# Moving phi's q + 1 to POOL, q's PSUM copy to ACT and low parts to DVE in an attention-and-MLP kernel

## The chip, the cores and the metric

The kernel runs on one core of a Trainium2 chip. The metric is the device time of one execution in microseconds (us). The engines of the core work at the same time and take their own queues in order: PE (TensorE, matmuls and transposes), DVE (VectorE), ACT (ScalarE), POOL (GpSimd) and SP, which issues the loads and stores. An instruction that waits holds up everything behind it in its engine's queue.

## The reference

Inputs are float32; B, H, S, D = 4, 8, 576, 64. First comes causal attention mixed with a linear memory, then two MLPs with 512 x 2048 and 2048 x 512 weights over the 2304 tokens:

```python
scores = np.where(causal, -1e9, q @ k.T / sqrt(D))      # per batch and head
local = softmax(scores) @ v
q_p = phi(q)                                  # phi(x) = (x if x > 0 else exp(x) - 1) + 1
mem_out = (q_p @ M_prev) / (q_p @ z_prev + 1e-6)
x = g * mem_out + (1 - g) * local             # g = sigmoid(beta), one value per head
x = x.transpose(0, 2, 1, 3).reshape(B * S, H * D)
h = x @ w_in;  x = (h * tanh(softplus(h))) @ w_out         # first MLP
h = x @ w_in2; out = (h * sigmoid(h)) @ w_out2             # second MLP
```

## The kernel before

Attention goes by 16 pairs of heads. A pair loads q, k and v (two buffers each); PE transposes q and k through PSUM, and the copies out of PSUM make `kT` (ACT, `Tkh`) and `qT` (DVE, `Tqh`). Scores are made in four bands of rows (`s4` to `s1`, and `s0` for the first 64 rows). DVE adds the mask and finds the extremum (`r`, line 562), ACT takes the exponential with the sum as its accumulator (`e`, line 586), DVE takes two small steps on the sum (`a` at line 616, `d` at 618), POOL scales the probabilities (`n`, line 601). PE transposes them (`X`), ACT and DVE copy them out, and PE multiplies by v (`V`, line 674).

Beside this, the memory part makes phi(q) as min(exp(q), 1) against q + 1: `phe` (ACT, exp), `phu` (ACT, q + 1, line 512), `phf` (DVE, line 513), then `phz` (POOL, product with z, line 515), `phr` (DVE, its sum, line 517), three small DVE steps and `phm` (POOL, line 522).

Both MLPs work in split precision: an operand is held as a high part, which is a cast to fp32r on ACT, and a low part, which is the operand less the high part. A product is three matmuls (lines 843 to 845 and 880). The tokens are cut into 6 blocks of 384 and the inner width of 2048 into 16 slices, in 4 quarters of 4 slices. A unit is one slice of one block: `in` (12 matmuls), `si` (ACT, the activation, line 858), `gh` (ACT, its high part, line 859), `gl` (DVE, its low part, line 860), `out` (12 matmuls in the first MLP, 9 in the second, line 880). Between `in` and `out` of one unit PE does other units' matmuls; there are three PSUM banks for `in` and five for `out`. The sums of a quarter are drained to `xT` (ACT for the first quarter, DVE after that, line 897).

There are 64 weight pieces (two MLPs x 16 slices x in and out). The loaded weights are put through bit steps on DVE (`abs` and `b0` to `b3`, lines 761 to 776, 128 x 512), then `hi` on ACT (line 784) and `lo` on POOL (line 788). The first quarter of the first MLP has 8 pieces, and their buffers exist from the start; the buffers for the next pieces and for the blocks of x open when attention's buffers close. Low parts of x (`xl`, line 829) are on POOL, but for two on DVE; there are 24 for each MLP.

The order on every engine comes from a planner (`Steps.plan`), which goes through all steps with a duration and an engine for each, and takes the ready step with the earliest latest-start time. `PERIOD` sets the due times of the pairs, and `SHIFT` adds a fixed time to the latest start of whole groups of steps. The planned order is then written out; the chip keeps it on each engine.

Of the kernel before, what the change touches and what calls it, by code (L numbers as in the profile page):

```python
# [21 lines left out]
AF = mybir.ActivationFunctionType  # L22
# [229 lines left out]
def pair_steps():  # L252
# [2 lines left out]
    for nm, d in (("nk", 1.6), ("nq", 1.7), ("nv", 3.1)):  # L255
        E("ld" + nm, "S", d, [], 2.7)
    E("phe", "A", act(640, False), ["ldnq"])
    E("phu", "A", act(640, False), ["ldnq"])
    m.group("t", ("Tk", "P", 0.44, ["ldnk"]), [("Tkh", "A", act(512), ["Tk"])])
    E("phf", "D", dve(640), ["phe", "phu"])  # L260
    m.group("t", ("Tq", "P", 0.44, ["ldnq"]), [("Tqh", "D", dve(512), ["Tq"])])
    E("phz", "G", 1.57, ["phf"])
    E("phr", "D", dve(640), ["phz"])
    E("pha", "D", 0.08, ["phr"])
# [71 lines left out]
class Attn:  # L336
# [162 lines left out]
    def steps(self, p):  # L499
# [9 lines left out]
        mid = slice(ST, S)  # L509

        f["phe"] = lambda: nc.scalar.activation(self.get(p, "e"), s["nq"], AF.Exp)
        f["phu"] = lambda: nc.scalar.activation(self.get(p, "u"), s["nq"], AF.Identity, bias=1.0)
        f["phf"] = lambda: nc.vector.scalar_tensor_tensor(  # L513
            out=s["e"], in0=s["e"], scalar=1.0, in1=s["u"], op0=ALU.min, op1=ALU.max)
        f["phz"] = lambda: nc.gpsimd.tensor_tensor(
# [13 lines left out]
        f["Tp"] = lambda: T("e")  # L529

        f["Tkh"] = lambda: self.hi(G("kT")[:, mid], s["Tnk"])
        f["Tqh"] = lambda: self.vec(G("qT"), s["Tnq"])
        f["Tph"] = lambda: [self.hi(G("W0")[R[j], j, mid], s["Te"][R[j], :]) for j in range(2)]

        def Ts():
# [192 lines left out]
class Weights:  # L728
# [13 lines left out]
    def steps(self, n):  # L742
        job = self.jobs[n]
        ph, i, part = job
        nc = self.nc

        def s_load():
            t = self.stg.tile([P, DM, 2], I32, tag="stg", name="stg")
            src = self.pairs[ph][part].bitcast(I32)
            if part == 0:  # L750
                nc.sync.dma_start(
                    t.rearrange("p (c f) x -> p c (f x)", c=KC),
                    src[:, 2 * i * P:2 * (i + 1) * P].rearrange("(c p) f -> p c f", p=P))
            else:
                nc.sync.dma_start(t.rearrange("p f x -> p (f x)"), src[i * P:(i + 1) * P, :])
            self.raw[job] = t

        def s_abs():
            c = self.stg.tile([P, DM], F32, tag="val", name="val", bufs=self.VALS)
            self.val[job] = c  # L760
            nc.vector.tensor_scalar(
                c.bitcast(U32), self.raw[job][:, :, 1].bitcast(U32), 0x7FFFFFFF, None, op0=ALU.bitwise_and)

        def s_bits(n):
            t, c = self.raw[job], self.val[job]
            cu = c.bitcast(U32)
            lo, hi = t[:, :, 0].bitcast(U32), t[:, :, 1].bitcast(U32)
            if n == 0:
                nc.vector.tensor_scalar(c, c, LEAST, MOST, op0=ALU.max, op1=ALU.min)
            elif n == 1:  # L770
                nc.vector.tensor_scalar(cu, cu, 3, 0x3FFFFFFF, op0=ALU.logical_shift_left, op1=ALU.bitwise_and)
            elif n == 2:
                nc.vector.scalar_tensor_tensor(
                    out=cu, in0=lo, scalar=29, in1=cu, op0=ALU.logical_shift_right, op1=ALU.bitwise_or)
            else:
                nc.vector.scalar_tensor_tensor(  # L776
                    out=lo, in0=hi, scalar=0xC0000000, in1=cu, op0=ALU.bitwise_and, op1=ALU.bitwise_or)

        def s_hi():
            k = i % SLOTS  # L780
            pool = self.fix if k < GC else self.late
            w = pool.tile([P, 2, DM], F32R, tag=f"w{k}{part}", name=f"w{k}{part}")
            self.W[job] = w
            nc.scalar.copy(w[:, 0, :], self.raw[job][:, :, 0].bitcast(F32))  # L784

        def s_lo():
            w = self.W[job]
            nc.gpsimd.tensor_tensor(  # L788
                w[:, 1, :], self.raw[job][:, :, 0].bitcast(F32), w[:, 0, :].bitcast(F32), op=ALU.subtract)
        bits = {f"b{n}": lambda n=n: s_bits(n) for n in range(4)}  # L790
        return dict(ld=s_load, abs=s_abs, hi=s_hi, lo=s_lo, **bits)

    def register(self, m, due, last):

        m.cap.update({"W.raw": 2, "W.val": self.VALS})
        for n, job in enumerate(self.jobs):
            ph, i, part = job
            f = self.steps(n)
            k = i % SLOTS
            ring = f"W.{k}{part}"  # L800
            m.cap[ring] = 1
            J = lambda x: ("W", job, x)
            t = due(job)
            slow = 0.2 if ph == 0 and i < GC else 0.0
            for x, e, d, deps in (("ld", "S", 3.8, []), ("abs", "D", 0.465, ["ld"]), ("b0", "D", 0.465, ["abs"]),
                                  ("b1", "D", 0.465, ["b0"]), ("b2", "D", 0.735, ["b1"]), ("b3", "D", 0.78, ["b2"]),
                                  ("hi", "A", 0.57, ["b3"] + (["open1"] if k >= GC else [])),
                                  ("lo", "G", 1.38, ["hi"])):
                m.add(J(x), e, d + (slow if e == "D" else 0.0), [y if y == "open1" else J(y) for y in deps], f[x], t)
            m.hold("W.raw", job, [J("ld")], [J("lo")], order=n)  # L810
            m.hold("W.val", job, [J("abs")], [J("b3")], order=n)
            m.hold(ring, job, [J("hi")], last(job), order=n)


class Moe:
# [5 lines left out]
    def split_x(self, ph, t, kc):  # L821
# [4 lines left out]
            nc.scalar.copy(self.xh[t][:, kc], self.xT[:, kc, ts])  # L826

        def lo():
            self.lo_engine(ph, t, kc).tensor_tensor(  # L829
                self.xl[t][:, kc], self.xT[:, kc, ts], self.xh[t][:, kc].bitcast(F32), op=ALU.subtract)  # L830
        return hi, lo

# [67 lines left out]
        r = t * TB + d * P  # L900
        self.nc.sync.dma_start(self.out[r:r + P, :], self.part(1, t, d))

    def lo_engine(self, ph, t, kc):
        return self.nc.vector if ph == 0 and t == 0 and kc % 2 else self.nc.gpsimd

    def open(self, n):

        tc, ctx = self.tc, self.ctx
# [17 lines left out]
    def register(self, m, base, ends, step=4.17):  # L926
# [6 lines left out]
        for t in range(NB):  # L933
            for kc in range(KC):
# [1 line left out]
                f = self.split_x(0, t, kc)  # L936
                heads = [(b * KC + kc, v) for b in range(t * TB // SEQ, ((t + 1) * TB - 1) // SEQ + 1) for v in ends]
                m.add((k, "h"), "A", 0.413, ["open%d" % (t // 3)] + heads, f[0], due[0, t, 0])
                e = self.lo_engine(0, t, kc) is self.nc.gpsimd
                m.add((k, "l"), "G" if e else "D", 0.955 if e else 0.466, [(k, "h")], f[1], due[0, t, 0])  # L940
        for n, u in enumerate(U):
            ph, t, i = u
            g = i // GC
# [26 lines left out]
            if i % GC == GC - 1:  # L970
                for d in range(nd):
# [11 lines left out]
                    if g == NG - 1 and ph == 0:  # L983
                        f = self.split_x(1, t, d)
                        z = ("z", t, d)
                        m.add((z, "h"), "A", 0.413, [k], f[0], due[1, t, 0])
                        m.add((z, "l"), "G", 0.955, [(z, "h")], f[1], due[1, t, 0])
                    elif g == NG - 1:
                        m.add((k, "st"), "S", 0.5, [k], lambda t=t, d=d: self.store(t, d), due[u] + 4)

# [10 lines left out]
        self.w.register(m, wdue, wlast)  # L1001


PERIOD = 9.921
SHIFT = {
# [19 lines left out]
}  # L1025


# [75 lines left out]
```

## Time and profile before

| what | us |
|---|---|
| median of 3 executions | 1046.67 (1046.45 to 1046.94) |
| the profiled execution, its own time | 1046.64 |
| its span in the trace | 1044.8 |
| PE busy | 1015.3 |
| DVE busy | 584.3 |
| ACT busy | 461.5 |
| POOL busy | 291.6 |

The span runs from the first to the last instruction in the trace, and 1.84 us of the execution lie around it. Busy times of several engines overlap. Matmuls are pipelined, so that a busy PE is not always PE at its peak rate. In an instruction's row `out<-in` gives the tiles by their names, and the brackets at its end hold the engine's idle time just before it and what ended that.

### The profile page before, as it was taken

The page shows a single profiled execution, that of the slowest core. Times are in us where ns is not written, and L with a number is a line of the kernel's source. Part 1 is how long each engine was busy: PE and PEld are TensorE (multiplying, and loading weights), DVE is VectorE, ACT ScalarE, POOL GpSimd, SP SyncE. Part 2 cuts the span into 40 slices and gives each one's busy share as a digit, 9 for nine tenths or more (in the row PEclk, how much of TensorE's full clock was granted, in tenths as well). Part 3 has the DMA queues.
Part 4 walks back from the last instruction along what each step waited for, and adds up shares of the span by engine and source line. Part 5 has one row for each costly group of instructions (what it writes and reads, how often), then busy time and mean ns, then how long its engine had stood idle before and what let it go on. Part 6 is the DMA issues. An engine that isn't in the chain of part 4 may idle for free.

```text
span 1044.8 us, 15751 instructions
## 1 busy us (share of the span) xinstructions
PE 1015.3 (97%) x5824; PEld 902.3 (86%) x5824; DVE 584.3 (56%) x1398; ACT 461.5 (44%) x1071; POOL 291.6 (28%) x303
## 2 busy tenths in 40 slices
PE   6999999988999999999999999999999999999998
PEld 4666666677999999999999999899999999998897
DVE  6999999999724732672278238512752372212222
ACT  6899898983424322332234334324422332222221
POOL 4887778787201200210024234101200120000000
PEclk9999999999999999999999999999999999999999
DMA  6433343122302300220031002100300120000011
GB/s 135 101 92 82 92 102 93 46 67 68 102 1 61 101 1 1 82 81 1 1 101 61 1 21 81 61 1 21 118 24 1 41 81 1 1 1 31 31 61 61
DMA packets 85309, 55.03 MB, mean 53 GB/s; under 512 B 61936, under 2 KB 78320, under 8 KB 85232
## 3 DMA queue, kind: packets, MB, share of 16 engines
q1 hardware_dynamic: 84032, 53.73, 18.2%
q8 instruction: 46, 0.75, 0.3%
q10 hardware_dynamic: 1200, 0.30, 0.1%
q14 instruction: 31, 0.25, 0.1%
HBM read 49.29 MB, written 4.72 MB: 52 GB/s over the span
## 4 chain that ended last, share of the span: by engine, by line
PE 80%; DVE 10%; POOL 4%; ACT 3%; issue 2%; DMA 1%; SPq 0%; POOLq 0%; ACTq 0%; DVEq 0%
PE acc L880 37%; PE hp L843 12%; PE hp L844 12%; PE hp L845 12%; DVE sm L562 3%; POOL xl L829 2%; PE ps_x L674 2%; PE ps_s L569 2%; DVE h L484 2%; ACT P L586 2%; PE ps_t L638 1%; DVE z L616 1%; DVE e L513 1%; PE ps_t L489 1%; DMA nq<-in_q_dram 1%
## 5 line engine op out<-in xcount | busy, mean ns | idle before, releaser
L858 ACT ACTIVATE a<-hp 128x384 f32<-128x384 f32 x192 | 94.5, 492 | 469.5 <-PE hp L845 469.4
L860 DVE TENSOR_TENSOR gl<-a,gh 128x384 fp32r<-128x384 f32 x192 | 116.4, 606 | 320.6 <-ACT gh L859 320.1
L843 PE MATMUL hp<-xh,w 128*128 128x384 f32 x768 | 258.9, 337 | 0.0
L844 PE MATMUL hp<-xl,w 128*128 128x384 f32 x768 | 258.5, 337 | 0.0
L845 PE MATMUL hp<-xh,w 128*128 128x384 f32 x768 | 258.5, 337 | 0.0
L788 POOL TENSOR_TENSOR w<-stg,w 128x512 fp32r<-128x512 f32 x64 | 86.6, 1354 | 474.5 <-ACT w L784 341.1
L880 PE MATMUL acc<-gh,w 128*128 128x384 f32 x768 | 212.1, 337 | 1.5 <-ACT gh L859 1.5
L880 PE MATMUL acc<-w,gh 128*128 128x512 f32 x576 | 180.4, 394 | 0.0
L843 PEld LDWEIGHTS hp<-xh,w 128*128 128x128 f32 x768 | 144.2, 188 | 4.5 <-issue 0.3
L844 PEld LDWEIGHTS hp<-xl,w 128*128 128x128 f32 x768 | 144.2, 188 | 4.2 <-DVE xl L829 0.2
L845 PEld LDWEIGHTS hp<-xh,w 128*128 128x128 f32 x768 | 144.2, 188 | 0.0
L880 PEld LDWEIGHTS acc<-gh,w 128*128 128x128 f32 x768 | 140.6, 188 | 1.8 <-ACT gh L859 1.8
L880 PE MATMUL acc<-gl,w 128*128 128x384 f32 x384 | 130.2, 339 | 7.0 <-DVE gl L860 7.0
L880 PEld LDWEIGHTS acc<-w,gh 128*128 128x128 f32 x576 | 106.9, 188 | 17.4
L897 DVE TENSOR_TENSOR xT<-acc,xT 128x384 f32<-128x384 f32 (+1 forms) x126 | 73.9, 612 | 83.6 <-PE acc L880 83.6
L880 PE MATMUL acc<-w,gl 128*128 128x512 f32 x288 | 113.8, 395 | 0.2 <-DVE gl L860 0.2
L601 POOL TENSOR_SCALAR P<-P,z,g 128x448 f32<-128x448 f32 (+3 forms) x128 | 94.0, 746 | 31.1 <-DVE z L618 17.3
L859 ACT CAST gh<-a 128x384 fp32r<-128x384 f32 x192 | 98.6, 513 | 5.4
L586 ACT ACTIVATE P<-sm,m 128x576 f32<-128x576 f32 (+4 forms) x144 | 83.7, 583 | 8.8 <-DVE m L562 6.7
L880 PEld LDWEIGHTS acc<-gl,w 128*128 128x128 f32 x384 | 72.1, 188 | 9.5 <-DVE gl L860 9.4
L784 ACT CAST w<-stg 128x512 fp32r<-128x512 f32 x64 | 42.3, 661 | 68.9 <-DVE stg L776 62.3
L880 PEld LDWEIGHTS acc<-w,gl 128*128 128x128 f32 x288 | 54.1, 188 | 14.0 <-DVE gl L860 1.4
(80 smaller groups left out, 1131.2 us busy)
## 6 DMA issues: line engine op xcount, KB each, us to landing
stg<-in_moe_w_in_dram SPq DMA_DIRECT2D x32, 512.0 KB, 3.7
stg<-in_moe_w_out_dram SPq DMA_DIRECT2D x32, 512.0 KB, 3.5
out_dram<-xT SPq DMA_DIRECT2D x18, 256.0 KB, 2.0
nq<-in_q_dram SPq DMA_DIRECT2D x32, 128.0 KB, 2.6
nv<-in_v_dram SPq DMA_DIRECT2D x32, 128.0 KB, 2.7
nk<-in_k_dram SPq DMA_DIRECT2D x30, 128.0 KB, 2.7
z<-in_z_prev_dram SPq DMA_DIRECT2D x4, 256.0 KB, 4.4
nq<-in_q_dram SPq DMA_DIRECT2D x16, 32.0 KB, 2.5
```

Source lines behind the costliest of these rows:

```text
L586: nc.scalar.activation(G(f"P{i}")[:, 1 - j if i else 1], s[f"sm{i}{j}"], AF.Exp, bias=s[f"m{i}"][:, j:j + 1], scale=-1.0, accum_out=G(f"z{ ...
L601: f[f"n{i}{j}"] = lambda i=i, j=j: nc.gpsimd.tensor_scalar(s[f"P{i}"][:, 1 - j], s[f"P{i}"][:, 1 - j], s[f"z{i}"][:, j:j + 1], self.g1[:, ...
L784: nc.scalar.copy(w[:, 0, :], self.raw[job][:, :, 0].bitcast(F32))
L788: nc.gpsimd.tensor_tensor(w[:, 1, :], self.raw[job][:, :, 0].bitcast(F32), w[:, 0, :].bitcast(F32), op=ALU.subtract)
L843: nc.tensor.matmul(hp, lhsT=wh, rhs=xh, start=(kc == 0), stop=False)
L844: nc.tensor.matmul(hp, lhsT=wh, rhs=xl, start=False, stop=False)
L845: nc.tensor.matmul(hp, lhsT=wl, rhs=xh, start=False, stop=(kc == KC - 1))
L858: f["si"] = lambda: nc.scalar.activation(self.new(u, "a", TB), self.hp[u], fn)
L859: f["gh"] = lambda: nc.scalar.copy(self.new(u, "gh", TB, F32R), g("a"))
L860: f["gl"] = lambda: nc.vector.tensor_tensor(self.new(u, "gl", TB, F32R), g("a"), g("gh").bitcast(F32), op=ALU.subtract)
L880: nc.tensor.matmul(o, lhsT=a, rhs=b, start=(first and k == 0), stop=(last and k == 2))
L897: nc.vector.tensor_tensor(part, acc, part, op=ALU.add)
```

## The change

Four kinds of step change their engine: `phu` goes from ACT to POOL (as a multiply-add with constants), `Tqh` from DVE to ACT, the low parts of x from POOL to DVE, and the low parts of weights from POOL to DVE, but for the 8 pieces of the first quarter of the first MLP. The planner's durations follow. `PERIOD` goes from 9.921 to 8.000, nearly all of the old entries of `SHIFT` have new values, and some 110 entries are added: for steps of the MLPs (`M`, `dr`, `z`) and for single weight pieces (`Wj`, `Wg`).

```diff
-    E("phu", "A", act(640, False), ["ldnq"])
+    E("phu", "G", 0.9, ["ldnq"])
...
-    m.group("t", ("Tq", "P", 0.44, ["ldnq"]), [("Tqh", "D", dve(512), ["Tq"])])
+    m.group("t", ("Tq", "P", 0.44, ["ldnq"]), [("Tqh", "A", act(512), ["Tq"])])
...
-        f["phu"] = lambda: nc.scalar.activation(self.get(p, "u"), s["nq"], AF.Identity, bias=1.0)
+        f["phu"] = lambda: nc.gpsimd.tensor_scalar(
+            self.get(p, "u"), s["nq"], 1.0, 1.0, op0=ALU.mult, op1=ALU.add)
...
-        f["Tqh"] = lambda: self.vec(G("qT"), s["Tnq"])
+        f["Tqh"] = lambda: self.hi(G("qT"), s["Tnq"])
...
-            nc.gpsimd.tensor_tensor(
+            eng = nc.gpsimd if ph == 0 and i < GC else nc.vector
+            eng.tensor_tensor(
                 w[:, 1, :], self.raw[job][:, :, 0].bitcast(F32), w[:, 0, :].bitcast(F32), op=ALU.subtract)
...
-                                  ("lo", "G", 1.38, ["hi"])):
+                                  ("lo",) + (("G", 1.38) if ph == 0 and i < GC else ("D", 0.6)) + (["hi"],)):
...
-            self.lo_engine(ph, t, kc).tensor_tensor(
+            nc.vector.tensor_tensor(
                 self.xl[t][:, kc], self.xT[:, kc, ts], self.xh[t][:, kc].bitcast(F32), op=ALU.subtract)
...
-                e = self.lo_engine(0, t, kc) is self.nc.gpsimd
-                m.add((k, "l"), "G" if e else "D", 0.955 if e else 0.466, [(k, "h")], f[1], due[0, t, 0])
+                m.add((k, "l"), "D", 0.466, [(k, "h")], f[1], due[0, t, 0])
...
-                        m.add((z, "l"), "G", 0.955, [(z, "h")], f[1], due[1, t, 0])
+                        m.add((z, "l"), "D", 0.466, [(z, "h")], f[1], due[1, t, 0])
...
-PERIOD = 9.921
+PERIOD = 8.000
```

## Rows read from the trace of the kernel before

**Rows 1.** The page: busy time and instructions of each engine; DVE's busy tenths in slices.
```profile
PE 1015.3 (97%) x5824; PEld 902.3 (86%) x5824; DVE 584.3 (56%) x1398; ACT 461.5 (44%) x1071; POOL 291.6 (28%) x303
...
DVE  6999999999724732672278238512752372212222
```

**Rows 2.** Busy time by stretch: length, PE, PEld, DVE, ACT, POOL; granted clock, DMA share, GB/s.
```profile
20.00:220.00 200.00, 191.31 (x1418) 126.05 (x1416) 191.92 (x740) 179.73 (x507) 151.50 (x178) 1.00 0.36 85
220.00:270.00 50.00, 41.51 (x238) 37.24 (x237) 45.95 (x47) 26.72 (x60) 35.90 (x29) 1.00 0.26 82
270.00:560.00 290.00, 290.00 (x1661) 290.00 (x1661) 146.01 (x252) 93.83 (x186) 39.42 (x30) 1.00 0.15 48
560.00:660.00 100.00, 99.79 (x555) 96.71 (x554) 56.10 (x85) 40.05 (x79) 33.39 (x29) 1.00 0.14 42
```

**Rows 3.** What ended PE's waits, 220 to 270 us: total, times, longest.
```profile
PE acc L880 <- DVE gl L860: 7.0, 6, 2.6
```

**Rows 4.** Instructions in order of time, 247 to 254 us, one engine after the other.
```profile
247.73 0.52 ACT L859 CAST gh<-a 128x384 fp32r<-128x384 f32 x1
...
247.78 4.91 POOL L829 TENSOR_TENSOR xl<-xT,xh 128x384 fp32r<-128x384 f32 x4
...
248.13 1.12 DVE L769 TENSOR_SCALAR val<-val 128x512 f32<-128x512 f32 x1
...
251.94 1.30 DVE L776 SCALAR_TENSOR_TENSOR stg<-stg,val 128x512 uint32<-128x512 uint32 x1
253.16 0.55 DVE L860 TENSOR_TENSOR gl<-a,gh 128x384 fp32r<-128x384 f32 x1
...
253.76 0.44 PE L880 MATMUL acc<-gl,w 128*128 128x384 f32 x1 [2.62 <-DVE gl L860]
```

**Rows 5.** Two DVE lines in 220:262, then in 290:560: ns least/median/most, first and last start.
```profile
L769 DVE TENSOR_SCALAR val<-val x5: 1124/1239/1541, 225.5 to 254.1; 128x512 f32<-128x512 f32 x5
...
L860 DVE TENSOR_TENSOR gl<-a,gh x7: 546/1342/1371, 231.8 to 261.9; 128x384 fp32r<-128x384 f32 x7
...
L769 DVE TENSOR_SCALAR val<-val x22: 419/428/1556, 327.3 to 553.0; 128x512 f32<-128x512 f32 x22
...
L860 DVE TENSOR_TENSOR gl<-a,gh x64: 548/558/1367, 290.1 to 556.3; 128x384 fp32r<-128x384 f32 x64
```

**Rows 6.** Groups of instructions by line and shape, whole span: busy us, mean ns.
```profile
L484 DVE COPY qT<-ps_t 128x512 f32<-128x512 f32 x16 | 10.9, 681 | 2.5 <-PE ps_t L489 2.5
...
L481 ACT COPY kT<-ps_t 128x512 f32<-128x512 f32 x16 | 9.2, 575 | 1.1 <-PE ps_t L489 1.1
...
L512 ACT ACTIVATE u<-nq 128x640 f32<-128x640 f32 x16 | 11.8, 737 | 2.0 <-DMA nq<-in_q_dram 1.4 <-DVE c L517 0.6
...
L601 POOL TENSOR_SCALAR P<-P,z,g 128x576 f32<-128x576 f32 x32 | 26.9, 848 | 16.0 <-DVE z L618 9.8 <-ACT P L586 2.6 <-ACT h L481 2.0
...
L829 POOL TENSOR_TENSOR xl<-xT,xh 128x384 fp32r<-128x384 f32 x46 | 54.4, 1211 | 37.6 <-ACT xh L826 37.5
...
L788 POOL TENSOR_TENSOR w<-stg,w 128x512 fp32r<-128x512 f32 x64 | 86.6, 1354 | 474.5 <-ACT w L784 341.1 <-DVE xT L897 120.5 <-PE hp L845 8.9
```

**Rows 7.** Instructions in order of time, POOL and DVE, near 74 and near 88 us.
```profile
73.84 2.48 POOL L601 TENSOR_SCALAR P<-P,z,g 128x192 f32<-128x192 f32 x3
...
74.28 0.83 DVE L513 SCALAR_TENSOR_TENSOR e<-e,u 128x640 f32<-128x640 f32 x1
...
88.42 1.55 POOL L515 TENSOR_TENSOR u<-e,z 128x640 f32<-128x640 f32 x1
...
88.47 1.53 DVE L616 TENSOR_SCALAR z<-z 128x2 f32<-128x2 f32 x1
```

**Rows 8.** The chain that ended last, by line: of 20 to 205 us, then of 222 to 270 us.
```profile
by line: DVE sm L562 16.8%; DVE h L484 8.9%; ACT P L586 8.2%; PE ps_s L569 7.2%; PE ps_x L674 6.8%; DVE z L616 6.4%; PE ps_t L638 5.3%; issue 4.2%; DVE e L513 4.0%; DVE W L484 3.3%; DVE c L517 2.8%; ACT W L481 2.2%; PE ps_t L489 2.0%; POOL 
...
by line: POOL xl L829 50.6%; issue 20.9%; POOL w L788 13.7%; DMA stg<-in_moe_w_out_dram 7.3%; PE acc L880 4.5%; ACT xh L826 1.9%; DVE gl L860 1.2%; POOLq L829 0.2%; POOLq L788 0.1%; DVE val L761 0.1%; DVEq L761 0.0%
```

**Rows 9.** The first MLP matmul, instructions of PE in order of time.
```profile
222.11 0.45 PE L843 MATMUL hp<-xh,w 128*128 128x384 f32 x1
```

More of the change, by code (lines that the diff above doesn't have):

```diff
@@ L901, in store @@
         self.nc.sync.dma_start(self.out[r:r + P, :], self.part(1, t, d))
-    def lo_engine(self, ph, t, kc):
-        return self.nc.vector if ph == 0 and t == 0 and kc % 2 else self.nc.gpsimd
     def open(self, n):
```

59 rows, old and new, of the table SHIFT are left out of this document.

## The prediction

> **What bounds the kernel now.** I read the page first, then a table of busy time by stage, then what ended PE's idle time, then single instructions in the stretch where PE idles.
>
> The page says PE 97% [rows 1], but that is a mean over stages with different limits. The slices show DVE full to about 250 us and then mostly idle [rows 1]. The table by stage [rows 2] makes three stages of it. In attention (20 to 220 us) DVE is busy 191.92 of 200 us, the highest of all engines once one remembers that PE's matmuls overlap; ACT has 179.73 and POOL 151.50. From 270 to 560 us PE is busy 290.00 of 290 and DVE 146.01 of it: the MLPs run at PE's rate, and nothing that happens on DVE, ACT or POOL there shows. Between them (220 to 270 us) PE is busy 41.51 of 50, so 8.5 us are lost. What ended the waits says to whom: 7.0 us of them to gl on DVE [rows 3].
>
> One of these waits, followed down [rows 4]: ACT finished gh at 248.25 (247.73 + 0.52). The gl that needs it started only at 253.16, and PE stood 2.62 us for it. In between DVE, which takes its queue in order, did four bit steps of a weight, from 248.13 (1.12 us) to 253.2 (the last 1.30). All that time POOL ran four xl in a row. The same steps are shorter where POOL is quiet: the 1.239 us median of one of them in 220 to 262 us is 0.428 later on, and gl itself goes from 1.342 to 0.558 [rows 5]. So while POOL runs a two-input subtraction, DVE's instructions on SBUF take two to three times as long, and gl is late behind them. The chain of this stretch names the same culprit: half of it is xl on POOL [rows 8]. The first MLP matmul runs at 222.11 [rows 9].
>
> **The change part by part.**
>
> *q's copy out of PSUM, DVE to ACT.* DVE loses 16 x 0.681 = 10.9 us; ACT gains 16 copies of the shape of kT's, 0.575 each = 9.2 us [rows 6]. On ACT the copy waits for PE's transposes; the exps are queued behind it, POOL's scaling and the PE transposes behind those. The scores wait for it as they did for DVE's.
>
> *phi's q + 1, ACT to POOL.* ACT loses 16 x 0.737 = 11.8 us [rows 6], so in sum ACT has 2.6 us less: about 177 us where it had 179.7. POOL gains 16 one-input instructions of 640 columns. No row shows one; the nearest is the scaling of P, 848 ns for 576 columns, and the two-input product of the same size, 1.55, is a bound from above [rows 6, 7]. I take 0.9, 14.4 us in all: POOL goes from 151.5 to about 166 of 200 [rows 2], still the emptiest engine. On POOL it waits for q's load, with the scaling of P queued behind it; the loads are prefetched a pair or more ahead, so I price the wait at nothing; without that cover it is 1 to 2 us for a pair.
>
> What it costs DVE is the open term. Against a two-input POOL instruction DVE simply waits: a step on two columns took 1.53 because the product u started just before it. Against the one-input scaling, DVE's two-input max took 0.83 [rows 7] and it was POOL that took 0.83 for each of three instructions of 192 columns, as long as it takes for 576. So the price lies between 0 and 0.9 us each (14.4 us). I take 0.1, about 2 us in all, nearest to the second pair, since phu is of that kind. The Trainium skill ("SBUF — State Buffer", Who interferes with whom) speaks against this step: a POOL instruction and a DVE instruction that needs the shared port pair exclude each other for a whole instruction, and whichever starts second waits. By that rule read strictly the whole 14.4 us could be lost. The trace agrees on the waiting itself (1.53 us), but shows the wait falling on POOL as often as on DVE when POOL's instruction is a one-input one.
>
> Attention's sum on DVE: -10.9 + 2 = -8.9 us of 191.9. If DVE alone set the pace, at the same 96%, the stage would shorten by 9.3. But ACT would then be 93% busy, and of the chain of 20 to 205 us the DVE lines that the row shows make 42%; ACT's exps, PE and issue are in it too [rows 8]. Bounds 0 and 10.9 (no contention); I take **-7 us**.
>
> *Low parts of x, POOL to DVE.* Of the first set (six blocks of four), 22 subtractions of 1.211 us leave POOL around 220 to 260 us [rows 6] and two are on DVE already; on DVE each costs a gl's 0.558 [rows 5], 12.3 us. *Low parts of weights.* 56 of 64 move; POOL loses 1.354 each, DVE gains at most 0.558 x 512/384 = 0.74 each. In 220 to 270 us that is some 6 instructions, 4.4 us. Against these 16.7 us, DVE's instructions there stop being stretched: 7 gl x 0.78 = 5.5 us, and 5 weights x 5 steps at 0.7 to 0.8 (the step shown loses 0.81) = about 18. So DVE goes from 45.95 of 50 [rows 2] to about 39. It has slack for the first time, and in the example the four steps between gh and gl shrink from 4.9 us to about 2 (in the ratio 0.428 to 1.239), which is most of the 2.62 that PE waited. Of the 8.5 us I take **-7 us** back; bounds 0 (gl still queued late) and 8.5.
>
> On DVE each low part now waits for its cast on ACT, where POOL waited before; behind it in DVE's queue stands the next gl, and PE waits for that. In the MLP stage some 50 such waits are new. DVE is half idle there [rows 2] and a single gl took up to 1.367 us [rows 5] without any PE idle, so there is 0.8 us to spare at the least. I cost it at nothing. The second set of low parts of x (24, between the two MLPs) lies under a PE that idles 0.2 us of 100 [rows 2]: nothing either. No transfer is added; a weight's staging buffer comes free after the low part, now earlier by 0.6 us, in a stage where nothing waits for loads on PE.
>
> *Period and shifts.* They only reorder queues. The order can't be read from them; I cost the reordering at nothing on average, and it is the reason for most of the range.
>
> **Rivals.**
> 1. *ACT and POOL take over in attention* (0.20). DVE gets its 9 us, but the exps behind the new copy come later, and the stage keeps its length. For: ACT 180 of 200 already, less than half of the chain surely DVE's. Against: DVE's idle is only 8 us of 200, and ACT's load falls by 2.6. Time: -7 alone, 1039.6.
> 2. *Early weights move out of attention* (0.12). The eight weights of the first quarter are prepared mostly in the DVE-bound stage, at least 5 x 0.428 = 2.1 us of DVE each by the unstretched step [rows 5]. With room on DVE after 220 us an order can leave four of them to it: 8.6 us more, 1024.0. For: the MLP's first units use them one after the other, 4 us apart. Against: what is left to DVE there again stands before gl.
> 3. *The port takes what the copy gave* (0.06). phu blocks DVE for its whole length: -10.9 + 14.4 = +3.5 in attention, -7 after it: 1043.1.
> 4. *No change* (0.04). Rival 1, and gl stays behind the weight steps in the order: 1046.6.
> 5. *Slower* (0.10). In the MLP stage the low parts hold up DVE's queue: a subtraction waits for a cast that on ACT stands behind a si, which waits for PE; gl comes late and PE stops. It decides when 56 weights cost more than 14 us, 0.25 us each. If half of them cost 0.7: 28 x 0.7 = 20, so 1052. For: waits of 2.6 us of just this kind exist [rows 3, 4]. Against: they vanish from 270 us on, where gl was still stretched at times.
>
> **How the numbers follow.** The profiled execution took 1046.64 us (span 1044.8 and 1.84 around it), the median 1046.67, so the sum is made on either. Likeliest (0.48): -7 - 7 = -14, **1032.6 us**, own range 1026 to 1039 by the bounds of the two terms. With the rivals: 1022 to 1043 leaves out rival 5, rival 4, half of rival 3 and the far part of rival 2, about 0.2. What a measurement can tell from no change is 0.2%, 2.1 us: faster 0.48 + 0.20 + 0.12 + 0.06 = 0.86, same 0.04, slower 0.10.
>
> **What would show it.** Right: in attention DVE still the fullest engine, and the first MLP matmul some 7 us earlier than 222 us; in the 50 us after it PE idle under 2 us, bit steps near 0.43 us and gl near 0.56; from there to the end the same length as before. Wrong: PE waits for gl spread over the MLP stage (rival 5); a first MLP matmul still near 222 us with ACT above 93% (rival 1) or with DVE's small steps stretched beside q + 1 (rival 3). If the attention stage loses more than 10.9 us, the order did it, and this working has missed it.

## The result, and the profile after

The changed kernel takes 1037.59 us (median of 4; 1037.50 to 1037.68) against 1046.80 for the kernel before: ratio 0.9913, interval 0.9895 to 0.9930. That is 9.2 us less, where 14 were forecast. The profiled execution took 1037.68 us, its span 1035.9. All times here and below are medians of fast executions: one of the fourth experiment (1412.41 us, at a granted clock of 0.657) and one of the eleventh (4412.15 us) were slow and are left out.

The page of the changed kernel, engines' busy time and then DVE's and POOL's tenths in slices:

```profile
PE 1012.4 (98%) x5824; PEld 902.0 (87%) x5824; DVE 582.7 (56%) x1484; ACT 458.4 (44%) x1071; POOL 172.9 (17%) x217
...
DVE  6999999987725723672367448413742562222222
...
POOL 6888887840000000000000000000000000000000
```

POOL is silent from the tenth slice on; DVE's total is as before, 582.7 where it was 584.3 [rows 1], although it took over 102 subtractions (46 of x and 56 of weights). Busy time by stretch of the changed kernel, columns as in [rows 2]:

```profile
20.00:220.00 200.00, 187.79 (x1398) 123.13 (x1396) 192.02 (x741) 176.58 (x506) 161.96 (x193) 1.00 0.38 93
220.00:270.00 50.00, 49.97 (x304) 47.23 (x304) 38.53 (x74) 31.03 (x69) 0.00 (x0) 1.00 0.21 65
270.00:560.00 290.00, 290.00 (x1660) 290.00 (x1659) 147.36 (x275) 93.19 (x185) 0.00 (x0) 1.00 0.15 48
560.00:660.00 100.00, 100.00 (x558) 98.03 (x557) 61.54 (x120) 40.57 (x80) 0.00 (x0) 1.00 0.14 43
```

The second row is the gain: PE's idle of 8.5 us in 220 to 270 us [rows 2] is 0.03. The first row is where the other half of the forecast was to come from, and it didn't: DVE is as busy as before (192.02 against 191.92), and PE did 20 instructions fewer by 220 us. The first MLP matmul comes 0.45 us later than in [rows 9]:

```profile
222.56 0.44 PE L845 MATMUL hp<-xh,w 128*128 128x384 f32 x1
```

What took the place of 10.9 us of copies on DVE? Two groups of 0 to 222 us, first of the kernel before, then of the changed one (the same lines of the program, moved by one):

```profile
L769 DVE TENSOR_SCALAR val<-val 128x512 f32<-128x512 f32 x7 | 3.8, 536 | 0.0
...
L518 DVE TENSOR_SCALAR c<-c 128x10 f32<-128x10 f32 x16 | 2.8, 172 | 0.0
```

```profile
L770 DVE TENSOR_SCALAR val<-val 128x512 f32<-128x512 f32 x10 | 4.7, 471 | 0.0
...
L519 DVE TENSOR_SCALAR c<-c 128x10 f32<-128x10 f32 x16 | 6.5, 406 | 0.2
```

The new order puts more of the weights' bit steps into attention (ten of this one where there were seven; all five kinds together take 28.1 us where they took 24.6), a small step of the memory part takes more than twice as long (+3.7 us), and the step on the sums takes 22.9 us where it took 21.3.

What ended PE's waits in 205 to 270 us of the changed kernel (total, times, longest). The 7.0 us for gl [rows 3] are gone:

```profile
PE ps_t L545 <- ACT h L481: 0.5, 1, 0.5
PE ps_t L639 <- DVE z L617: 0.3, 1, 0.3
```

DVE's lines in 220 to 262 us of the changed kernel (ns least/median/most, as in [rows 5]), among them the low parts of x and of weights:

```profile
L770 DVE TENSOR_SCALAR val<-val x4: 422/428/430, 243.9 to 259.7; 128x512 f32<-128x512 f32 x4
...
L862 DVE TENSOR_TENSOR gl<-a,gh x8: 551/559/559, 229.7 to 258.6; 128x384 fp32r<-128x384 f32 x8
...
L831 DVE TENSOR_TENSOR xl<-xT,xh x24: 541/549/560, 220.5 to 238.6; 128x384 fp32r<-128x384 f32 x24
...
L790 DVE TENSOR_TENSOR w<-stg,w x5: 693/693/694, 239.1 to 259.1; 128x512 fp32r<-128x512 f32 x5
```

These steps are no longer stretched: the bit step that had a median of 1.239 us has 0.428, gl 0.559 where it was 1.342. The two moved attention steps, in groups by line and shape (busy us, mean ns), ACT's q copy from 0 to 230 us and POOL's q + 1 from the whole span:

```profile
L481 ACT COPY qT<-ps_t 128x512 f32<-128x512 f32 x16 | 9.3, 580 | 1.9 <-PE ps_t L489 1.9
...
L512 POOL TENSOR_SCALAR u<-nq 128x640 f32<-128x640 f32 x16 | 11.7, 730 | 3.7 <-DMA nq<-in_q_dram 3.2 <-DVE m L563 0.5
```

### The profile page after: what moved, and what is told of

Same layout as the page of the kernel before. It is cut to its first block, busy times and chain, and to the rows that moved or that the text cites. A ratio compares the mean times of both kernels' runs of the same rounds, so it can differ in the third digit from the quotient of the medians.

```text
span 1035.9 us, 15735 instructions
## 1 busy us (share of the span) xinstructions
PE 1012.4 (98%) x5824; PEld 902.0 (87%) x5824; DVE 582.7 (56%) x1484; ACT 458.4 (44%) x1071; POOL 172.9 (17%) x217
## 4 chain that ended last, share of the span: by engine, by line
PE 84%; DVE 11%; ACT 3%; issue 1%; DMA 0%; POOL 0%; SPq 0%; ACTq 0%; POOLq 0%; DVEq 0%
PE acc L882 39%; PE hp L845 13%; PE hp L847 13%; PE hp L846 13%; DVE sm L563 4%; PE ps_x L675 2%; DVE h L484 2%; PE ps_s L570 2%; DVE z L617 2%; ACT P L587 1%; PE ps_t L639 1%; PE ps_t L489 1%; DVE W L484 1%; ACT W L481 1%; DVE e L514 0%
## 5 line engine op out<-in xcount | busy, mean ns | idle before, releaser
L862 DVE TENSOR_TENSOR gl<-a,gh 128x384 fp32r<-128x384 f32 x192 | 107.0, 557 | 343.1 <-ACT gh L861 342.9
L602 POOL TENSOR_SCALAR P<-P,z,g 128x320 f32<-128x320 f32 (+3 forms) x128 | 92.5, 732 | 25.0 <-DVE z L619 15.0
L570 PE MATMUL ps_s<-kT,qT 64*128 64x288 f32 (+3 forms) x320 | 62.5, 468 | 3.3 <-DVE m L563 1.4
L563 DVE CUSTOM_DVE_ANT_0 sm<-ps_s,mask 128x320 f32<-128x320 f32 (+3 forms) x128 | 58.2, 472 | 2.3 <-PE ps_s L570 1.1
```

The costliest lines, as they stand in the source:

```text
L563: nc.vector.tensor_tensor_reduce(out, ps, mask, -0.125, init, ALU.add, ALU.min, acc)
L570: nc.tensor.matmul(ps, lhsT=s["qT"][R[j], qcols(i)], rhs=s["kT"][R[j], k0 + cols.start:k0 + cols.stop], start=True, stop=True)
L602: f[f"n{i}{j}"] = lambda i=i, j=j: nc.gpsimd.tensor_scalar(s[f"P{i}"][:, 1 - j], s[f"P{i}"][:, 1 - j], s[f"z{i}"][:, j:j + 1], self.g1[:, ...
L862: f["gl"] = lambda: nc.vector.tensor_tensor(self.new(u, "gl", TB, F32R), g("a"), g("gh").bitcast(F32), op=ALU.subtract)
```

## Experiments

All are compared with the kernel before on the same chip, in five rounds each. The kernel before took 1046.80, 1046.84 and 1046.86 us in the three sets of runs (one to four, five to eight, nine to twelve). "Order kept" means that the planner gets the old engines and durations, so that every engine's queue keeps its order, and only the call that is written out changes its engine.

### One: the low parts alone, order of before

```diff
-            self.lo_engine(ph, t, kc).tensor_tensor(
+            nc.vector.tensor_tensor(
...
-            nc.gpsimd.tensor_tensor(
+            eng = nc.gpsimd if ph == 0 and i < GC else nc.vector
+            eng.tensor_tensor(
```

> The kernel before with its order kept; only the low parts (24 + 24 of x, 56 of weights) run on DVE instead of POOL. Theory A (the whole gain is PE's idle in 220 to 270 us, and it comes from taking POOL off the port that DVE's instructions share with it): about 8 us faster, 1038 to 1040, PE's busy time in 220 to 270 us at 49 or more of 50, first MLP matmul still near 222 us. Rival B (the new order did it; with the old one gl stays behind the weights' bit steps, now with 16 us more of DVE work): 0 to 3 us faster, 1044 to 1047, PE still waiting for gl for over 5 us.

1036.55 us, ratio 0.9900 (0.9885 to 0.9915): 10.25 us faster, and about 1 us faster than the whole change. Busy time in 220 to 270 us of this kernel:

```profile
220.00:270.00 50.00, 49.22 (x295) 46.84 (x294) 45.30 (x89) 31.42 (x69) 2.90 (x2) 1.00 0.33 105
```

and all that is left of PE's waits there:

```profile
PE acc L881 <- DVE gl L861: 0.8, 2, 0.5
```

DVE is as full as before (45.30 against 45.95), but does 89 instructions where it did 47, and PE waits 0.8 us for gl in place of 7.0. Theory A holds; the gain is even above its range, since PE does 57 instructions more in this stretch, and a matmul here starts every 0.17 us: 9.9 us of work. This one part of the change gives all of its gain.

### Two: the two attention steps alone, order of before

```diff
-        f["phu"] = lambda: nc.scalar.activation(self.get(p, "u"), s["nq"], AF.Identity, bias=1.0)
+        f["phu"] = lambda: nc.gpsimd.tensor_scalar(
+            self.get(p, "u"), s["nq"], 1.0, 1.0, op0=ALU.mult, op1=ALU.add)
...
-        f["Tqh"] = lambda: self.vec(G("qT"), s["Tnq"])
+        f["Tqh"] = lambda: self.hi(G("qT"), s["Tnq"])
```

> The kernel before with its order kept; only phi's q + 1 runs on POOL and q's copy on ACT. Theory A (DVE's 10.9 us were really on the path of the attention stage, and the changed kernel gave them away again through its new order): 6 to 10 us faster, 1037 to 1041, first MLP matmul near 214 us. Rival B (the stage is not set by DVE's sum of work but by the waits between the engines): within 2.5 us of the kernel before, 1044 to 1049, with DVE idle more than before in 20 to 220 us. Rival C (q + 1 on POOL blocks DVE's port for its whole length): 2 to 5 us slower, 1049 to 1052, and DVE's small steps beside it stretched.

1048.91 us, ratio 1.0020 (1.0012 to 1.0029): 2.1 us slower. Attention, 20 to 220 us:

```profile
20.00:220.00 200.00, 189.56 (x1400) 124.65 (x1398) 184.69 (x718) 175.11 (x501) 159.87 (x190) 1.00 0.36 85
```

DVE's work falls by 7.2 us (the 14 copies that fell into this stretch took 9.5), and the time turns into idle: 15.3 us of the 200 in place of 8.1. Rival B, and against the forecast of 7 us. The run by itself doesn't exclude rival C, whose range begins at 2 us: in 0 to 225 us the two-column step on the sums took 22.9 us here and 21.3 in the kernel before. The seventh run takes q + 1 alone.

### Three: the changed kernel's order, low parts back on POOL

```diff
-            eng = nc.gpsimd if ph == 0 and i < GC else nc.vector
+            eng = nc.gpsimd
...
-            nc.vector.tensor_tensor(
+            (nc.vector if ph == 0 and t == 0 and kc % 2 else nc.gpsimd).tensor_tensor(
                 self.xl[t][:, kc], self.xT[:, kc, ts], self.xh[t][:, kc].bitcast(F32), op=ALU.subtract)
```

> The changed kernel with its order kept; the low parts are put back on POOL (two of x on DVE, as before). Theory A (the low parts' engine is the whole gain): 7 to 9 us slower than the changed kernel, 1045 to 1047, PE idle again by 6 us or more in 220 to 270 us. Rival B (the new order is): within 2 us of the changed kernel, 1036 to 1040.

1039.57 us, ratio 0.9934 (0.9921 to 0.9946): only 2.0 us slower than the changed kernel, and 9.3 us faster than the second run, which has the same engines in the old order. The stretch from 220 to 270 us, then DVE and POOL in order of time:

```profile
220.00:270.00 50.00, 48.52 (x292) 45.20 (x293) 26.02 (x37) 28.71 (x64) 30.95 (x28) 1.00 0.17 53
```

```profile
229.53 2.27 DVE L862 TENSOR_TENSOR gl<-a,gh 128x384 fp32r<-128x384 f32 x2 [4.18 <-ACT gh L861]
234.19 0.85 DVE L862 TENSOR_TENSOR gl<-a,gh 128x384 fp32r<-128x384 f32 x1 [2.39 <-ACT gh L861]
241.78 1.39 DVE L862 TENSOR_TENSOR gl<-a,gh 128x384 fp32r<-128x384 f32 x1 [6.73 <-ACT gh L861]
250.00 0.43 DVE L762 TENSOR_SCALAR val<-stg 128x512 uint32<-128x512 uint32 x1 [6.83 <-DMA stg<-in_moe_w_in_dram]
...
223.71 21.31 POOL L831 TENSOR_TENSOR xl<-xT,xh 128x384 fp32r<-128x384 f32 x20 [0.18 <-POOL xl L831]
```

POOL does twenty xl in a row and stretches gl just as before (1.39 us), but PE idles only 1.5 us. While those xl run, up to 245 us, the new order has no weight step between one gl and the next; the first comes at 250.00, when its load has landed, and takes 0.43 us. In the whole stretch DVE has 26 us of work where it had 46. So rival B holds, as theory A did in the first run: taking the weights' steps out of gl's way, or making them short, cures the same stall. Either is enough, and the change does both.

### Four: the changed kernel's order, attention steps back

The diff of the second run turned round, in the changed kernel.

> The changed kernel with its order kept; phi's q + 1 is put back on ACT and q's copy back on DVE. Theory A (the two moved steps are worth their DVE time, and the new order hides it): 7 to 11 us slower than the changed kernel, 1045 to 1049. Rival B (the stage is set by waits between engines, and DVE's work is not what it costs): within 3 us of the changed kernel, 1035 to 1041. Rival C (the port): 2 to 5 us faster, 1033 to 1036.

1040.51 us, ratio 0.9938 (0.9925 to 0.9952): 2.9 us slower than the changed kernel. That is rival B, at the edge of its 3 us, and far from theory A. In this order the two steps are worth 3 us; in the old one they cost 2. What in the new order suits them, no run isolates. The first run has the same engines in the old order and takes 1036.55: with the attention steps in their old places the new order costs 4.0 us.

### Five to seven: all engines in the old order, and each attention step alone

Each has the low parts on DVE and the order of before, as in the first run; the fifth has both attention steps moved too, the sixth only q's copy, the seventh only q + 1.

> The kernel before with its order kept and all four kinds of step on the engines of the changed kernel. Theory A (the two moved attention steps cost 2 us in the old order whatever follows): the 1036.6 of the low parts alone plus 2, 1038 to 1039.5, about 1 us slower than the changed kernel. Rival B (with POOL off the port after 220 us the late end of attention is covered): 1036 to 1037. Rival C (the new order costs more than it brings): under 1036.

> Order of before; low parts on DVE and q's copy on ACT, q + 1 left on ACT. ACT has 9.3 us more. Theory A (what costs time is ACT's queue: the copy stands in front of exps and of the copies that PE waits for): 2 to 6 us slower than the low parts alone, 1038.5 to 1042.5, with DVE waiting more for ACT's P. Rival B (DVE's time is what counts): 3 to 8 us faster than that, 1028 to 1033.

> Order of before; low parts on DVE and q + 1 on POOL, q's copy left on DVE. ACT has 11.8 us less. Theory A (q + 1 on POOL costs by the port and by POOL's queue): 1 to 4 us slower than the low parts alone, 1037.5 to 1040.5, DVE's small steps longer by 3 us or more in sum. Rival B (ACT's queue is what the stage waits for): 1 to 4 us faster, 1032.5 to 1035.5.

| kernel | us | against the first run |
|---|---|---|
| low parts alone (first run) | 1036.55 | |
| with both steps (fifth) | 1038.55 | +2.0 |
| with q's copy on ACT (sixth) | 1037.74 | +1.2 |
| with q + 1 on POOL (seventh) | 1037.38 | +0.8 |

The ratios to the kernel before are 0.9918 (0.9904 to 0.9931), 0.9911 (0.9898 to 0.9925) and 0.9909 (0.9895 to 0.9922). The parts add up: 0.8 + 1.2 = 2.0, and theory A of the fifth run holds. The changed kernel is 1 us below the fifth, and the two differ in the order alone. Differences of about 1 us are below what these intervals can tell apart (the first run's is 0.9885 to 0.9915), so that the sum may come out this well by luck; that neither step is worth several microseconds is plain.

Attention, 20 to 220 us, in the sixth run, and what DVE waited for in 20 to 200 us there; in the first run the same wait was 1.8 us, 6 times:

```profile
20.00:220.00 200.00, 189.09 (x1402) 125.28 (x1400) 183.55 (x724) 183.08 (x515) 149.82 (x176) 1.00 0.36 85
```

```profile
DVE z L616 <- ACT P L586: 6.8, 13, 0.9
```

DVE's 8.5 us of saved work come back as idle, 5.0 of them as waits for the exps, which now stand behind the copy in ACT's queue. These waits are theory A's; its range began at 1038.5, and the measured time misses it from below.

The seventh run, its attention stage and DVE's small step on the sums (0 to 225 us), and the same step in the first run:

```profile
20.00:220.00 200.00, 191.32 (x1406) 126.04 (x1404) 192.37 (x739) 170.96 (x489) 160.47 (x191) 1.00 0.36 85
```

```profile
L617 DVE TENSOR_SCALAR z<-z 128x2 f32<-128x2 f32 x64 | 21.8, 342 | 1.9 <-ACT P L587 1.5
```

```profile
L616 DVE TENSOR_SCALAR z<-z 128x2 f32<-128x2 f32 x64 | 21.9, 344 | 2.4 <-ACT P L586 2.0
```

POOL has 9.5 us more than in the first run (150.98) and ACT 8 less (179.04), and DVE's step on the sums is on average no longer than it was, where theory A asked for 3 us more; the time, too, is just below its range. That mean hides what single rows of POOL and DVE show:

```profile
41.36 0.73 POOL L512 TENSOR_SCALAR u<-nq 128x640 f32<-128x640 f32 x1
...
41.55 0.56 DVE L617 TENSOR_SCALAR z<-z 128x2 f32<-128x2 f32 x1
...
154.26 0.89 POOL L512 TENSOR_SCALAR u<-nq 128x640 f32<-128x640 f32 x1
...
154.49 1.33 DVE L514 SCALAR_TENSOR_TENSOR e<-e,u 128x640 f32<-128x640 f32 x1
```

The step on the sums has a median of 0.164 us in 20 to 220 us and the max (line 514) one of 0.826. Each of these two started behind a q + 1 and took 0.4 to 0.5 us longer. Five of the sixteen q + 1 have such a neighbour, and DVE lost some 1.8 us to them (an estimate: the time above the lower quartile of each kind). DVE is busy 582.9 us in the whole run, 581.7 in the first. So the port does cost something, about what the prediction took. The 8 us that ACT is freed of bring nothing.

### Eight: DVE's small step on the sums left out

```diff
-            f[f"a{i}"] = lambda i=i, n=n: nc.vector.tensor_scalar(
-                s[f"z{i}"][:, :n], s[f"z{i}"][:, :n], 1.0, 1e-9, op0=ALU.mult, op1=ALU.add)
+            f[f"a{i}"] = None
```

> Order of before; low parts on DVE, and the step that adds 1e-9 to the sums of the exponentials is left out (80 instructions, 23.6 us of DVE's attention work; the sums are 1 or more, so that float32 doesn't hold the 1e-9). Nothing else is moved. Theory A (DVE's work sets the attention stage, and the two moved steps failed only by what they put on ACT and POOL): 12 to 22 us faster than the low parts alone, 1014 to 1025. Rival B (waits between the engines set it, and DVE's work is no bound): 0 to 5 us faster, 1031 to 1037, with DVE idle by 15 us or more of 20 to 220 us.

1028.25 us, ratio 0.9820 (0.9807 to 0.9834): 8.3 us below the first run, between the theories. Attention, then the chain of 20 to 205 us by line:

```profile
20.00:220.00 200.00, 196.29 (x1477) 131.89 (x1474) 187.16 (x674) 186.39 (x524) 151.48 (x178) 1.00 0.38 90
```

```profile
by line: PE ps_s L569 20.1%; PE ps_x L673 16.7%; PE ps_t L637 16.6%; PE ps_t L489 7.1%; DVE sm L562 6.2%; POOL P L601 5.9%; ACT P L586 3.8%; issue 3.1%; DVE h L484 2.4%; POOL P L618 1.4%; ACT W L481 1.4%; PE ps_t L538 1.3%; PE ps_t L654 1.3
```

The step stands between an exp on ACT and POOL's scaling, and PE's transposes come after that. The first MLP matmul comes at 213.79 us, where the first run has it at 222.71. With the step gone, the chain is PE's: the scores, the transposes and the products with v make 60% of it where they made 21% [rows 8]. So 23.6 us taken from DVE brought 8.3, and then PE stopped it.

### Nine and ten: DVE work taken away and given to nobody

In the ninth run q's copy is left out on every engine (the scores read k's columns). In the tenth three of five bit steps are left out for the first eight weight pieces. Both have the low parts on DVE and the order of before.

```diff
-        f["Tqh"] = lambda: self.vec(G("qT"), s["Tnq"])
+        f["Tqh"] = None
...
-                    ps, lhsT=s["qT"][R[j], qcols(i)], rhs=s["kT"][R[j], k0 + cols.start:k0 + cols.stop],
+                    ps, lhsT=s["kT"][R[j], qcols(i)], rhs=s["kT"][R[j], k0 + cols.start:k0 + cols.stop],
```

```diff
-        bits = {f"b{n}": lambda n=n: s_bits(n) for n in range(4)}
+        bits = {f"b{n}": (lambda n=n: s_bits(n)) if n == 3 or ph or i >= GC else None for n in range(4)}
```

> Low parts on DVE, order of before, and q's copy out of PSUM left out on every engine (the scores take k's columns in its place, so the values are not the reference's). DVE loses 10.9 us, ACT gains nothing. Theory A (DVE's work is on the path, and moving the copy failed only because ACT's queue took it up): 5 to 9 us faster than the low parts alone, 1027.5 to 1031.5. Rival B (the copy is no part of what sets the stage, wherever it runs): 0 to 2 us faster, 1034.5 to 1036.5.

> Low parts on DVE, order of before, and three of the five DVE steps left out for the eight weight pieces of the first quarter of the first MLP (their values are not the reference's). DVE loses about 15 us that no step of attention waits for. Theory A (DVE's sum of work sets the stage): 6 to 9 us faster than the low parts alone, 1027.5 to 1030.5. Rival B (only what stands in a chain between the engines counts, and these steps fill gaps): within 2.5 us, 1034 to 1037.

Ninth: 1035.71 us, ratio 0.9893 (0.9880 to 0.9907), 0.8 below the first run. Tenth: 1033.52, ratio 0.9872 (0.9857 to 0.9887), 3.0 below. Attention in each, first the ninth:

```profile
20.00:220.00 200.00, 191.07 (x1416) 126.06 (x1418) 187.47 (x725) 179.18 (x507) 150.91 (x177) 1.00 0.36 85
```

```profile
20.00:220.00 200.00, 192.87 (x1442) 127.84 (x1439) 184.54 (x725) 181.81 (x513) 148.52 (x179) 1.00 0.37 87
```

The ninth decides the argument about q's copy in the old order. 10.9 us of copies taken from DVE, with nothing added anywhere, are worth 0.8 us: rival B, the copy was hardly on the path. (DVE's busy time falls by 5.7 us in the whole run, 581.7 to 576.0, since other steps of it took longer.) In the tenth, 13.9 us (the three steps' sum in 20 to 222 us of the first run: 5.7, 4.4 and 3.8) brought 3.0, just outside rival B's 2.5 and far from theory A's 6. DVE's time is worth between a fourteenth and a third of itself here, by where it stands.

### Eleven and twelve: the better version

The eleventh is the changed kernel without the step on the sums, order kept; the twelfth is the eighth with q + 1 on POOL.

> The changed kernel, order kept, without the step that adds 1e-9 to the sums. Theory A (as in the old order PE becomes the bound of attention): 1026 to 1030, with PE lines first in the chain of 20 to 220 us. Rival B (the new order costs attention time of its own): 1031 to 1035.

> Order of before; low parts on DVE, no 1e-9 step, and q + 1 on POOL. ACT, at 186 of 200 us without the 1e-9 step, loses 11.8 us. Theory A (PE is the bound by now): within 1.5 us of 1028.3. Rival B (ACT is): 2 to 6 us faster, 1022 to 1026. Rival C (POOL's queue is late with q + 1): 1 to 3 us slower, 1029.5 to 1031.5.

1029.25 us, ratio 0.9830 (0.9817 to 0.9843), and 1029.41, ratio 0.9833 (0.9820 to 0.9847). In the eleventh, theory A: PE's lines lead the chain of 20 to 205 us:

```profile
by line: PE ps_x L674 18.6%; PE ps_s L570 18.5%; PE ps_t L638 12.9%; DVE sm L563 7.7%; PE ps_t L489 6.2%; DVE h L484 4.7%; POOL P L602 3.2%; issue 2.7%; ACT P L587 2.4%; DMA stg<-in_moe_w_in_dram 2.3%; PE ps_t L539 1.8%; PE ps_t L545 1.5%; 
```

The twelfth is 1.2 us above the eighth, where theory A (within 1.5) and rival C (1 to 3) overlap; it is not the 2 to 6 us faster that ACT as the bound would give. So the eighth has the lowest median of all, 18.6 us below the kernel before and 9.3 below the changed one; the eleventh and twelfth lie within its interval. Its result is the same, since each sum contains the 1 of its own maximum and float32 doesn't hold 1e-9 beside it.

## Why the prediction was right and where it was wrong

The sign, the range and one of the two terms were right; the size, -14 against -9.2, was not. The likeliest branch (0.48), in which both stages shorten, didn't come: the time is inside the range because that is wide enough for one term to fail.

**The stretch after attention (-7): right, and somewhat too small.** The reading held step by step: xl on POOL stretched DVE's steps, gl stood behind them, PE waited. With the low parts on DVE the steps are short and the 8.5 us of idle are gone. The first run shows that this alone is worth 10.25 us. Idle time undercounts such a gain (7.7 us less idle, 9.9 us of matmuls more): in a run a matmul's record is 0.33 us long and the next starts after 0.17, and one that restarts PE has 0.44. The record of a restart is in [rows 4]; a run, in the changed kernel:

```profile
227.95 0.33 PE L847 MATMUL hp<-xh,w 128*128 128x384 f32 x1
228.12 0.33 PE L845 MATMUL hp<-xh,w 128*128 128x384 f32 x1
```

At each stall some 0.27 us of loss so count as busy (an estimate from these three). For the waits that are gone, seven less two, that is 1.4 us of the 2.2 between the two figures; the rest stays open. What the working missed is that the order could do it too (third run): it had the reordering at nothing on average, and with these engines it is worth 9.3 us (second against third run).

**The attention stage (-7): wrong.** The first MLP matmul of the changed kernel comes 0.45 us later, not 7 earlier. The failing step is the one that turned DVE's 8.9 us of saved work into 7 us of time because DVE was busy 96%. Measured on the old order, the two moved steps cost 2.1 us (second run), 1.2 by the copy and 0.8 by q + 1 (sixth and seventh); in the new one they bring 2.9 (fourth). DVE's busy time didn't fall in the changed kernel at all: more weight steps came into attention, and small steps got longer. The ninth run shows that the copy was hardly on the path: removing it altogether brings 0.8 us, and DVE idles more in its place. On ACT it stood in front of exps, and DVE's waits for those grew from 1.8 to 6.8 us. DVE's 96% was true and was no bound: it held weight steps that nothing in this stage waits for, and copies with slack. The Trainium skill ("Perfetto Trace Analysis", Identifying the Most-Contended Engine) would have led the same way, as it takes occupancy for VectorE, ScalarE and GpSimd as the measure and says to optimise the highest first. Read as a rule for what pays, it would have work taken off DVE show in the time; taking away 10.9 us of copies gave 0.8, and the measurement decides.

**Rival 1** (ACT and POOL take over) named the outcome, 1039.6, but its mechanism only in part: ACT was busy 176.58 of 200 us, 88%, where the sign for it was above 93%, and ACT freed of 8 us brought nothing either (seventh run). So no run shows a single engine as the bound before PE, which is 8 us behind (eighth run). That the waits between the queues, and so their order, set the stage is what is left; that the order alone can cost 4.0 us is shown (fourth run against first). **Rival 2** had the order move weight steps out of attention; it moved more in.

**The port (+2 of attention's sum): about right.** Beside q + 1 DVE lost some 1.8 us in the seventh run. The strict reading that the prediction took from the Trainium skill ("SBUF — State Buffer", Who interferes with whom), 14.4 us, doesn't happen here: beside eleven of the sixteen q + 1 no DVE step is clearly longer. But a one-input POOL instruction does hold up DVE, and that the wait falls on POOL as often was read from a single row.

**The other costs held.** A low part of x took 0.551 us on DVE (0.558 taken), one of a weight 0.693 (at most 0.74), q's copy on ACT 0.580 (0.575), q + 1 on POOL 0.73 (0.9). The 50 new waits in DVE's queue in the MLP stage cost PE nothing (290.00 of 290), so rival 5 didn't happen.

**The account:** 1046.80 - 10.25 (low parts) + 2.0 (attention steps) - 0.96 (new order) = 1037.59. It adds up by the way it is made, and its last term is not clear of noise (ratios 0.9918 and 0.9913, each within 0.0017). It depends on the way taken: from the new order's side the low parts are worth 2.0 and the attention steps 2.9, and the order itself is worth 9.3 us with the low parts on POOL, 1.0 with all moved, and -4.0 with the low parts alone moved.

**Open:** what in the new order makes the attention steps worth 3 us, and which single place in ACT's or POOL's queue costs the 1.2 and 0.8 us in the old one. The waits point to exps behind the copy, but no run moved only these.

## What to carry to other kernels

An engine that is 96% busy under a fixed order need not set the pace: before moving its work, take the piece away on every engine and see what that is worth, for a piece with slack is worth little wherever it runs. In a stage where PE idles, follow one wait down to the instructions that stand in the queue in front of the late one, and ask both why they are long and why they are in front; either cure may do, and the two don't add. Price a removed stall by the instructions that fit into it, not by idle time alone.

## What the runs showed of the hardware

A one-input POOL instruction of 640 columns took 0.73 us in the changed kernel, less than the 0.85 of the scaling of 576 columns with two scalars from memory [rows 6]. Such an instruction can hold up DVE: in the seventh run a two-column step that started 0.19 us behind one took 0.56 us (median 0.164). It happened beside five of sixteen, so that the mean of those steps didn't show it (342 ns, 344 without q + 1 on POOL). Two-input subtractions on POOL stretched gl to 1.39 us in the third run, as in [rows 5].
